# A fused adaLN, segment-memory attention and gated-MLP block: chunked weight loads, a rebuilt prologue and a fill rate per segment

## The chip, the cores and the metric

One Trainium2 chip, one core. The metric is device time in microseconds, lower is better: the median of several executions. Beside it there is one execution taken with the hardware profiler, which has a time of its own.

## The reference, cut to what matters

The block works on x of shape (1, 2048, 448): 16 heads of 28, four segments of 512 rows, and an MLP of width 1792. Everything is bf16 outside.

```python
mod = (silu(c) @ w_mod).reshape(1, 6, 1, -1)
sa, ca, ga, sb, cb, gb = mod[:, 0], mod[:, 1], ...
h = layernorm(x) * (1 + ca) + sa
q, k, v = h @ wq, h @ wk, h @ wv          # 4 segments, 16 heads
for s in range(4):
    p = softmax(q_s @ k_s.T * scale + causal_mask)
    a_dot = p @ v_s
    a_mem = (phi(q_s) @ M) / (phi(q_s) @ z + 1e-6)
    o_s = g * a_mem + (1 - g) * a_dot     # g = sigmoid(beta), per head
    M, z = M + phi(k_s).T @ v_s, z + phi(k_s).sum()
x = x + ga * (o @ wo)
h = layernorm(x) * (1 + cb) + sb
x = x + gb * ((sigmoid(h @ w_gate) * (h @ w_up)) @ w_down)
```

phi(t) is t + 1 above zero and exp(t) below.

## The kernel before, in words

All weights and all of x stay in SBUF. The work goes by the four segments of 512 rows (four tiles of 128 rows each). Heads go in four groups of four (hc), each head padded to 32 rows, so that one group fills 128 partitions.

The program is written in the order in which each engine shall run it; every engine (TensorE, VectorE, ScalarE, GpSimd called POOL, and SP, which only starts DMAs) takes its own instructions in that order and waits by semaphores. The order is made by hand in the main loop at the end. Its spine is the attention: for each segment s and head group hc three groups g of logits (`logits`, L386, with the exponential on ScalarE, L389, and the causal mask on POOL, L397), and after the first of them the product with v for the head group before (`pv`, L411, and L419 for the memory), with its ends on VectorE (L425 to L446). After each group `run_fill` takes other jobs from the queue `fill` until their costs, in ns, have used up the rate of that group. These jobs are the projections of q, k and v (`proj_qk` L311, `proj_v` L323), the memory update (`mem_update` L359), the Wo tiles (`wo_tile` L461, with the residual, L464, and the statistics of the second layer norm, L238), gate and up (`gate_up` L479 and L484) and down (`down` L493). A job has a planned cost: `MM, MV, TR = 216, 190, 60` ns for a matmul of 512 columns, one of 448, and a transpose. So a q or k projection costs 864, a v projection or a Wo tile 760, a gate/up pair 1728, a down tile 2660.

Work that should come some time later on another engine is put off by `later(ns, ...)`. A clock, counted up by the costs of what has been written so far, says when it is due; `need(tag)` forces what is not yet written. So a layer norm (`ln1_start`) is spread out: statistics at once, norm (L246) at 5200 to 6700, modulation (L257) at 14500 to 16000 ns after its start. For segments 2 and 3, and for the second layer norm, h is transposed by a DMA between the norm and the modulation (`norm_t`, L253, on SP); for segments 0 and 1 by TensorE (`pe_chunk`, L265 to L270). The transposes of phi(k) (L348) and of the attention's output (`otr`, L452), every load after the start and every store (L498) are SP's too, in one order.

The prologue loads x, the first two pieces of w_mod (`load_wm`, L113), wq, wk and wv, sets pads to zero on VectorE (L133 to L172), runs 24 warm-up matmuls (L562) on a zeroed tile, normalises segment 0, copies wq (ScalarE) and wk (VectorE) into the padded form (`pad_copy`, L573), computes two modulation vectors (`mod_cols`, L205, into `cp`) and transposes and modulates h (L265 to L270). Then two projections come, and the main loop. `load_wo` and the loads of w_gate, w_up and w_down are each one job of cost 0 in `fill`, with the two FFN matrices as one big DMA and one for the last 64 rows.

The rate of `run_fill` is 2400 ns for the first five head groups and (total − 15 × 2400) / 33 for the rest. The total leaves 9 gate/up jobs for the end (`TAIL_GU`). At the second head group of segments 1 to 3 the jobs of the segment before are added: four Wo tiles, what was left in the queue, down of the segment before that, the modulation (`h2_jobs`) and gate/up. After the loop the rest of the last two segments follows.

Of the kernel before, what the change touches and what calls it, by code (L numbers as in the profile page):

```python
# [17 lines left out]
def kernel(  # L18
# [34 lines left out]
    NWARM, TAIL_GU = 24, 9  # L53
# [13 lines left out]
    def m_f32(name):  # L67
        return ps_m.tile([P, 512], F32, tag="m", name=name)
# [32 lines left out]
    nc.sync.dma_start(c_col[:], c.rearrange("o (k p) -> p (o k)", p=KP))  # L101
    x_sb = const.tile([P, NSEG * TPS, D], BF16)

    def load_x(eng, t0, t1):
        eng.dma_start(x_sb[:, t0:t1, :], x_dram[t0 * P:t1 * P, :].rearrange("(t p) d -> p t d", p=P))

    load_x(nc.sync, 0, 2)
    load_x(nc.scalar, 2, 4)
    wmod_k = w_mod.rearrange("(k p) n -> p k n", p=KP)
# [30 lines left out]
    nc.vector.memset(wo_sb[:], 0.0)  # L140
    nc.vector.memset(wg_sb[LW:P, 3, :], 0.0)
    nc.vector.memset(wu_sb[LW:P, 3, :], 0.0)
# [15 lines left out]
    nc.gpsimd.memset(mhalf[:], -0.5)  # L158
    bmask = const.tile([P, NHC, 4, ME], BF16)
# [10 lines left out]
    qT_of = [const.tile([P, NHC, L], BF16, name=f"qT{s}") for s in range(3)]  # L170
    qT_of.append(qT_of[0])
    nc.vector.memset(qT_of[2][:, 0, :], 0.0)  # L172

# [3 lines left out]
    nc.vector.tensor_scalar(th[:], th[:], 0.5, 0.5, op0=ALU.mult, op1=ALU.add)  # L177
    silu = const.tile([KP, NK], BF16)
    nc.vector.tensor_tensor(silu[:], th[:], c_col[:], ALU.mult)
# [3 lines left out]
    def late_consts():  # L183
        nc.vector.tensor_copy(silu_bc[:], silu[:].rearrange("p (k o) -> p k o", o=1).to_broadcast([KP, NK, P]))
        for s in range(NSEG):
            nc.gpsimd.memset(vt_all[s][:, :, :, Dh:Dh + 1], 1.0)
        nc.scalar.activation(coef[:, 1, :], beta_t[:], AF.Tanh, scale=0.5)
        nc.vector.tensor_scalar(coef[:, 1, :], coef[:, 1, :], 0.5, 0.5, op0=ALU.mult, op1=ALU.add)
        nc.vector.tensor_scalar(coef[:, 0, :], coef[:, 1, :], -1.0, 1.0, op0=ALU.mult, op1=ALU.add)

        nc.gpsimd.memset(bmask[:], 1.0)
        for hs in range(4):
            nc.gpsimd.affine_select(out=bmask[:, :, hs, :], in_=bmask[:, :, hs, :], compare_op=ALU.is_ge,
                                    fill=0.0, base=-HP * hs, pattern=[[0, NHC], [0, ME]], channel_multiplier=1)
            nc.gpsimd.affine_select(out=bmask[:, :, hs, :], in_=bmask[:, :, hs, :], compare_op=ALU.is_ge,
                                    fill=0.0, base=HP * hs + Dh - 1, pattern=[[0, NHC], [0, ME]],
                                    channel_multiplier=-1)

    def mod_cols(jobs):
        cp = m_f32("cp")  # L200
        for j, vi in jobs:
            for kc in range(NK):
                for k in range(NK):
                    c0 = k * D + kc * P
                    nc.tensor.matmul(cp[:, vi * NK + kc:vi * NK + kc + 1], lhsT=wm[j][:, c0:c0 + P],  # L205
                                     rhs=silu[:, k:k + 1], start=(k == 0), stop=(k == NK - 1))
# [21 lines left out]
    class LN:  # L228
# [171 lines left out]
    def pv(s, hc):  # L400
# [24 lines left out]
        nc.vector.reciprocal(r1[:], accv[:, :, :, Dh])  # L425
        nc.vector.tensor_tensor(r1[:], r1[:], cb(0), ALU.mult)
# [14 lines left out]
        nc.vector.tensor_scalar(r2[:], memv[:, :, :, Dh], 1e-6, None, op0=ALU.add)  # L441
        nc.vector.reciprocal(r2[:], r2[:])
        nc.vector.tensor_tensor(r2[:], r2[:], cb(1), ALU.mult)
# [13 lines left out]
    def wo_tile(s, t):  # L457
# [12 lines left out]
        later(1500, lambda: ln.norm_t(t), ("ln2", s))  # L470

# [87 lines left out]
    wz = qT_of[2][:, 0, :]  # L559
    warm = ps_lg.tile([P, 4, 512], F32, tag="lg", name="warm")  # L560
    for _ in range(NWARM):
        nc.tensor.matmul(warm[:, 0, :], lhsT=ident[:], rhs=wz, start=True, stop=True)  # L562
    ln0 = LN([x_sb[:, t, :] for t in range(TPS)], ("1", 0))
    for t in range(TPS):
        ln0.stats(t)
    ln0.rstd(0, TPS)
    for t in range(TPS):
        ln0.norm(t)
# [36 lines left out]
    def load_wd():
        nc.sync.dma_start(wd_sb[:], B_w_down.rearrange("(fc p) n -> p fc n", p=P))

    fill.extend(sp(load_bw2) + j0[2:6] + sp(late_consts) + j0[6:10] + [ln1_start(2)] + j0[10:])
    fill.extend(sp(load_wo) + sp(load_wm3) + load_ffn(wg_sb, B_w_gate))
    fill.extend(ln1_pe_jobs(1) + m[0][0:1] + j1[:8] + [ln1_start(3)] + load_ffn(wu_sb, B_w_up) + m[1][0:1] + j1[8:] + [(1000, prep_b1)])  # L610
    fill.extend(sp(load_wd) + j2[:4] + m[0][1:] + j2[4:8] + [(2000, prep_b2)] + j2[8:] + m[1][1:])
# [5 lines left out]
    total = cost(fill) + sum(cost(wo_jobs(s) + h2_jobs(s) + gu_jobs(s)) for s in range(3)) \
        + sum(cost(down_jobs(s)) for s in range(2)) - TAIL_GU * 8 * MM
    early = 2400.0
    rate = lambda s, hc: early if s * NHC + hc < 5 else (total - 15 * early) / 33.0  # L620

    debt = 0.0
    for s in range(NSEG):
        for hc in range(NHC):
            prev = (s, hc - 1) if hc else (s - 1, NHC - 1)
            for g in range(3):
# [15 lines left out]
                debt = run_fill(rate(s, hc) + debt)  # L642
# [51 lines left out]
```

## Time and profile before

| | us |
|---|---|
| median of 3 runs | 284.12 (283.15 to 285.14) |
| the profiled execution, its own time | 282.85 |
| its span, from the first to the last instruction | 281.1 |
| TensorE (PE) busy | 250.8 |
| VectorE (DVE) busy | 187.4 |
| ScalarE (ACT) busy | 140.8 |
| GpSimd (POOL) busy | 70.8 |

All rows that follow are of the profiled execution, and their times count from its first instruction. PEld is TensorE's loading of weights, which runs beside its matmuls. SPq is the queue of SP. A row of the timeline has the start, the time that the merged instructions took, the engine, the line, the operation, output and inputs, the count, and in square brackets how long the engine had been idle before it and what released it. The granted clock is TensorE's, 1.00 for 2.4 GHz and 0.50 for 1.2 GHz.

### The profile page before, as it was taken

To read this page: it belongs to the slowest core of one execution; us is meant where nothing else is said; L and a number is where in the kernel's file an instruction comes from. 1 tells how busy PE (TensorE), PEld (TensorE's weight loads), DVE (VectorE), ACT (ScalarE), POOL (GpSimd) and SP (SyncE) were. 2 spreads that over 40 slices of the span, in tenths; PEclk is the share of its full clock that TensorE was granted. 3 is DMA by queue.
4 is the path that set the end of the run, shared out by engine and by line. 5 is a ranking of instruction groups with operands and counts; after the bars stand their busy time and mean duration, and the time that the engine had idled before them with its cause. 6 is when DMAs were issued, how large, how long until landed. Compare 5 with 4: busy or idle time off the path is not lost. (4 is left out here: it accounts for less than half of the span.)

```text
span 281.1 us, 5201 instructions
## 1 busy us (share of the span) xinstructions
PE 250.8 (89%) x2025; PEld 123.0 (44%) x2048; DVE 187.4 (67%) x426; ACT 140.8 (50%) x171; POOL 70.8 (25%) x127
## 2 busy tenths in 40 slices
PE   1989897983888999998797999889999999899995
PEld 0434453541453544544353554435545444344452
DVE  7578899910679778999655858976577493433321
ACT  2268798583365788765165667562662310133300
POOL 1109434331234034144312213521220040000000
PEclk9999998896699999999999999999999999999999
DMA  5998046699412001301211001141300012100001
GB/s 152 294 249 255 2 105 197 118 198 230 104 21 56 23 19 21 75 21 37 54 54 36 21 0 21 37 57 34 55 19 4 18 37 70 35 0 0 2 16 49
DMA packets 40848, 19.66 MB, mean 70 GB/s; under 512 B 29560, under 2 KB 39928, under 8 KB 40824
## 3 DMA queue, kind: packets, MB, share of 16 engines
q1 hardware_dynamic: 39608, 18.30, 29.2%
q10 hardware_dynamic: 1216, 1.03, 1.3%
q8 instruction: 16, 0.26, 0.4%
q14 instruction: 8, 0.07, 0.1%
HBM read 10.67 MB, written 1.84 MB: 44 GB/s over the span
## 5 line engine op out<-in xcount | busy, mean ns | idle before, releaser
L389 ACT ACTIVATE pT<-lg 128x2048 bf16<-128x2048 f32 (+1 forms) x48 | 76.5, 1594 | 48.6 <-PE lg L386 48.6
L397 POOL TENSOR_SCALAR_AFFINE_SELECT pT<-pT 128x512 bf16<-128x512 bf16 x64 | 43.9, 700 | 87.8 <-ACT pT L389 87.8
L487 DVE SCALAR_TENSOR_TENSOR fT<-tt,ups 128x512 bf16<-128x512 f32 x56 | 37.8, 683 | 35.9 <-PE ups L484 24.6
L479 PE MATMUL gps<-hT,wg_sb 128*128 128x512 bf16 x213 | 57.9, 380 | 3.5 <-DVE hT L257 2.6
L481 ACT ACTIVATE tt<-gps 128x512 f32<-128x512 f32 x56 | 33.0, 596 | 53.9 <-PE gps L479 49.4
L484 PE MATMUL ups<-hT,wu_sb 128*128 128x512 bf16 x219 | 56.6, 379 | 2.4 <-DVE t L439 1.5
L493 PE MATMUL dps<-wd_sb,fT 128*128 128x448 bf16 x224 | 44.2, 353 | 2.3 <-DVE fT L487 2.3
L484 PEld LDWEIGHTS <-wu_sb 128*128 128x128 bf16 x224 | 21.5, 98 | 30.1 <-DVE t L439 2.5
L479 PEld LDWEIGHTS <-wg_sb 128*128 128x128 bf16 x224 | 20.4, 97 | 28.9 <-issue 7.4
L493 PEld LDWEIGHTS <-fT 128*128 128x128 bf16 x224 | 21.4, 98 | 23.5 <-DVE fT L487 2.5
L497 DVE TENSOR_TENSOR ot<-dps,x_sb 128x448 bf16<-128x448 f32 x16 | 9.9, 622 | 23.3 <-PE dps L493 23.3
L411 PEld LDWEIGHTS <-pT 128*128 128x128 bf16 x640 | 18.4, 96 | 4.9 <-issue 2.0
L323 PE MATMUL pv<-wv_sb,hT 128*128 128x448 bf16 x64 | 14.7, 372 | 6.1 <-DVE kT L316 6.1
L238 DVE BATCH_NORM_STATS2 st<-x_sb 128x6 f32<-128x448 bf16 x32 | 19.7, 617 | 0.6
L311 PE MATMUL pq<-hT,wq_sb 128*128 128x512 bf16 x61 | 17.9, 391 | 2.5 <-DVE hT L257 1.3
L242 POOL TENSOR_SCALAR rs<-mv 128x1 f32<-128x1 f32 (+1 forms) x20 | 5.1, 255 | 59.0 <-DVE mv L239 59.0
L411 PE MATMUL acc<-vt,pT 128*128 128x29 bf16 x640 | 18.5, 175 | 1.4 <-ACT vt L325 1.4
L386 PE MATMUL lg<-qT,kT 28*128 28x512 bf16 (+3 forms) x256 | 17.6, 307 | 0.9 <-DVE kT L316 0.8
L311 PE MATMUL pq<-hT,wk_sb 128*128 128x512 bf16 x60 | 17.0, 392 | 1.1 <-ACT qT L314 0.7
L257 DVE TENSOR_SCALAR hT<-hT,cols 128x512 bf16<-128x512 bf16 x24 | 9.6, 447 | 12.4 <-DMA hT<-xn 12.3
L246 DVE TENSOR_SCALAR xn<-x_sb,mv,rs 128x448 bf16<-128x448 bf16 x32 | 15.3, 494 | 2.4 <-POOL rs L243 2.3
L243 POOL TENSOR_TENSOR rs<-rs,mhalf 128x1 f32<-128x1 f32 (+1 forms) x20 | 13.7, 683 | 1.7
(81 smaller groups left out, 232.6 us busy)
## 6 DMA issues: line engine op xcount, KB each, us to landing
wm<-in_w_mod_dram SPq DMA_DIRECT2D x5, 392.0 KB, 4.2
out_dram<-ot SPq DMA_DIRECT2D x16, 112.0 KB, 1.7
wd_sb<-in_B_w_down_dram SPq DMA_DIRECT2D x1, 1568.0 KB
x_sb<-in_A_x_dram SPq DMA_DIRECT2D x3, 448.0 KB, 5.5
wg_sb<-in_B_w_gate_dram SPq DMA_DIRECT2D x1, 1344.0 KB, 11.3
wu_sb<-in_B_w_up_dram SPq DMA_DIRECT2D x1, 1344.0 KB
wm<-in_w_mod_dram ACTq DMA_DIRECT2D x1, 392.0 KB, 6.1
wo_sb<-in_A_wo_dram SPq DMA_DIRECT2D x4, 98.0 KB
```

Source lines behind the costliest of these rows:

```text
L238: nc.vector.bn_stats(st[:], self.srcs[i])
L246: nc.vector.tensor_scalar(self.xn[:, i, 0:D], self.srcs[i], self.mv[:, i, 0:1], self.rs[:, i:i + 1], op0=ALU.subtract, op1=ALU.mult)
L311: nc.tensor.matmul(pq[:, 0:L], lhsT=head_cols(w_sb, k, hc), rhs=h[:, k, :], start=(k == 0), stop=(k == NK - 1))
L386: nc.tensor.matmul(lg[:, hs, wid:wid + nq], lhsT=kT[r, hc, kb * P:(kb + 1) * P], rhs=qT[r, hc, kb * P:L], start=True, stop=True, tile_posi ...
L389: nc.scalar.activation(pT[:, :, w0:w0 + wid], lg[:, :, 0:wid], AF.Exp, scale=scale)
L397: nc.gpsimd.affine_select(out=blk, in_=blk, compare_op=ALU.is_ge, fill=0.0, base=0, pattern=[[0, 4], [1, P]], channel_multiplier=-1)
L411: nc.tensor.matmul(accv[:, qb, hs, 0:ME], lhsT=pT[:, hs, c0:c0 + P], rhs=vt[:, kb, hc * 4 + hs, 0:ME], start=(kb == 0), stop=(kb == qb))
L479: nc.tensor.matmul(gp[:, 0:L], lhsT=wg_sb[:, k, fs], rhs=h[:, k, :], start=(k == 0), stop=(k == NK - 1))
L481: nc.scalar.activation(tt[:], gp[:, 0:L], AF.Tanh, scale=0.5)
L484: nc.tensor.matmul(up[:, 0:L], lhsT=wu_sb[:, k, fs], rhs=h[:, k, :], start=(k == 0), stop=(k == NK - 1))
L487: nc.vector.scalar_tensor_tensor(ft[:], tt[:], 1.0, up[:, 0:L], op0=ALU.add, op1=ALU.mult)
L493: nc.tensor.matmul(dp[:, 0:D], lhsT=fT_of[(s, fc)][:, t * P:(t + 1) * P], rhs=wd_sb[:, fc, :], start=(fc == 0), stop=(fc == NFC - 1))
```

## The change

Four parts. The prologue: c is loaded after x, the warm-up's tile is zeroed first, three memsets go from VectorE to POOL, the rstd is done for two tiles at a time, the modulation vectors and two more warm-ups come ahead of the transposes, the transposes go tile by tile, and a third projection stands ahead of the loop. The loads: w_gate and w_up are loaded in four chunks of 128 rows (the last of 64) each and w_down in four chunks, one after every second job (`spread`). The end of a Wo stage: from segment 2 on the Wo tiles alternate with the jobs that were left, and the modulation of the second layer norm is put off by 6500 to 7700 ns after the last Wo tile instead of standing in the queue after down. The fill rate: 2400 ns until the second head group of segment 1; from there it is fixed per segment, so that 4, 4 and 9 gate/up jobs are left when the segment ends. Besides, the two gates of the output are inverted once, with one small operation less per head group from segment 1 on.

```diff
...
-    NWARM, TAIL_GU = 24, 9
+    NWARM, EARLY, KEEP = (20, 2), 2400.0, (0, 4, 4, 9)
...
-    nc.sync.dma_start(c_col[:], c.rearrange("o (k p) -> p (o k)", p=KP))
...
     load_x(nc.sync, 0, 2)
     load_x(nc.scalar, 2, 4)
+    nc.sync.dma_start(c_col[:], c.rearrange("o (k p) -> p (o k)", p=KP))
...
+    wz = qT_of[2][:, 0, :]
+    nc.vector.memset(wz, 0.0)
...
-    nc.vector.memset(wo_sb[:], 0.0)
-    nc.vector.memset(wg_sb[LW:P, 3, :], 0.0)
-    nc.vector.memset(wu_sb[LW:P, 3, :], 0.0)
...
     nc.gpsimd.memset(mhalf[:], -0.5)
+    nc.gpsimd.memset(wo_sb[:], 0.0)
+    nc.gpsimd.memset(wg_sb[LW:P, 3, :], 0.0)
+    nc.gpsimd.memset(wu_sb[LW:P, 3, :], 0.0)
...
+        nc.vector.tensor_scalar(coef[:], coef[:], 1e-30, None, op0=ALU.max)
+        nc.vector.reciprocal(coef[:], coef[:])
...
-        nc.vector.reciprocal(r1[:], accv[:, :, :, Dh])
-        nc.vector.tensor_tensor(r1[:], r1[:], cb(0), ALU.mult)
+        nc.vector.tensor_tensor(r1[:], accv[:, :, :, Dh], cb(0), ALU.mult)
+        nc.vector.reciprocal(r1[:], r1[:])
...
-        nc.vector.tensor_scalar(r2[:], memv[:, :, :, Dh], 1e-6, None, op0=ALU.add)
+        nc.vector.scalar_tensor_tensor(r2[:], memv[:, :, :, Dh], 1e-6, cb(1), op0=ALU.add, op1=ALU.mult)
         nc.vector.reciprocal(r2[:], r2[:])
-        nc.vector.tensor_tensor(r2[:], r2[:], cb(1), ALU.mult)
...
         later(1500, lambda: ln.norm_t(t), ("ln2", s))
+        if t == TPS - 1:
+            for kc in range(NK):
+                later(6500 + 400 * kc, lambda kc=kc: ln.modulate(kc, 2), ("ln2", s))
...
-        def mods():
-            need(("ln2", s))
-            for kc in range(NK):
-                ln2_of[s].modulate(kc, 2)
-        return [(0, mods)]
+        return [(0, lambda: need(("ln2", s)))]
...
+    warm_up(NWARM[0])
+    ln0 = LN([x_sb[:, t, :] for t in range(TPS)], ("1", 0))
+    for t in range(TPS):
+        ln0.stats(t)
+        if t % 2:
+            ln0.rstd(t - 1, t + 1)
+        if t == 1:
+            silu_ops()
+    mod_cols(((0, 0), (1, 1)), False)
+    warm_up(NWARM[1])
+    pts = [m_bf16("lntr") for _ in range(NK)]
     for k in range(NK):
         pad_copy(nc.scalar, wq_sb, wq_st, k)
-        pad_copy(nc.vector, wk_sb, wk_st, k)
-    mod_cols(((0, 0), (1, 1)))
+    for t in range(TPS):
+        ln0.norm(t)
+        if t == 1:
+            for k in range(NK):
+                pad_copy(nc.vector, wk_sb, wk_st, k)
+            mod_evac(((0, 0), (1, 1)))
+        for kc in range(NK):
+            nc.tensor.transpose(pts[kc][:, t * P:(t + 1) * P], ln0.xn[:, t, kc * P:(kc + 1) * P], ident[:])
+    for kc in range(NK):
+        ln0.pe_evac(pts[kc], kc, 0)
...
-    for c, fn in j0[:2]:
+    for c, fn in j0[:3]:
...
+    early_loads = [load_wo, lambda: load_x(nc.sync, 3 * TPS, 4 * TPS), load_wm3] \
+        + [piece(wg_sb, B_w_gate, k) for k in range(NK)] + [piece(wu_sb, B_w_up, k) for k in range(NK)]
+    fill.extend(sp(load_bw2))
+    fill.extend(spread(j0[3:6] + sp(late_consts) + j0[6:10] + [ln1_start(2)] + j0[10:] + ln1_pe_jobs(1) + m[0][0:1]
+                       + j1[:8], early_loads, 2))
+    fill.extend([ln1_start(3)] + m[1][0:1] + j1[8:] + [(1000, prep_b1)])
+    fill.extend(spread(j2[:4] + m[0][1:] + j2[4:8] + [(2000, prep_b2)], [piece_wd(f, min(f + 4, NFC)) for f in range(0, NFC, 4)], 2))
+    fill.extend(j2[8:] + m[1][1:])
...
-                    fill.extend(wo_jobs(s - 1) + tail)
+                    for w in wo_jobs(s - 1):
+                        fill.append(w)
+                        if tail and s > 1:
+                            fill.append(tail.pop(0))
+                    fill.extend(tail)
...
+                    pace[0] = (cost(fill) - KEEP[s] * 8 * MM) / (12 if s < 3 else 9)
-                debt = run_fill(rate(s, hc) + debt)
+                debt = run_fill(pace[0] + debt)
...
```

`piece` loads 128 rows of a weight matrix, `piece_wd` four of the 14 blocks of w_down, both on SP; `spread(jobs, steps, 2)` puts one load after every second job.

## Rows read from the trace of the kernel before

**Rows 1.** The page's first part: busy us, share of the span, instructions.

```profile
PE 250.8 (89%) x2025; PEld 123.0 (44%) x2048; DVE 187.4 (67%) x426; ACT 140.8 (50%) x171; POOL 70.8 (25%) x127
```

**Rows 2.** Busy time by stages: stage, length, PE, PEld, DVE, ACT, POOL, clock, DMA, GB/s.

```profile
28.00:30.20 2.20, 1.12 (x18) 0.88 (x16) 2.13 (x7) 2.12 (x3) 1.35 (x3) 1.00 0.00 0
45.00:47.50 2.50, 1.18 (x7) 0.30 (x4) 2.35 (x8) 2.50 (x6) 1.52 (x2) 1.00 0.69 158
47.50:51.00 3.50, 3.24 (x10) 0.93 (x11) 3.39 (x7) 1.53 (x3) 2.23 (x4) 0.52 1.06 354
...
61.20:64.60 3.40, 2.04 (x52) 1.43 (x51) 0.00 (x0) 2.25 (x5) 0.63 (x1) 1.00 1.02 306
64.60:74.90 10.30, 4.68 (x29) 2.53 (x27) 4.12 (x13) 2.77 (x4) 1.22 (x2) 0.51 1.15 180
...
77.80:125.20 47.40, 44.87 (x415) 22.16 (x416) 40.49 (x91) 33.49 (x41) 14.95 (x24) 1.00 0.17 35
125.20:138.00 12.80, 10.16 (x100) 5.23 (x98) 12.00 (x30) 5.07 (x5) 6.27 (x13) 1.00 0.14 32
138.00:151.00 13.00, 11.40 (x105) 5.82 (x105) 7.53 (x18) 6.01 (x5) 3.59 (x6) 1.00 0.18 49
...
174.00:187.00 13.00, 11.29 (x104) 5.40 (x102) 11.92 (x29) 6.41 (x7) 5.85 (x12) 1.00 0.17 40
...
224.00:243.00 19.00, 17.69 (x90) 8.61 (x90) 11.77 (x26) 1.19 (x2) 3.31 (x8) 1.00 0.18 47
```

**Rows 3.** The timeline, VectorE and TensorE, around 70 us.

```profile
69.79 0.74 DVE L257 TENSOR_SCALAR hT<-hT,cols 128x512 bf16<-128x512 bf16 x2 [12.35 <-DMA hT<-xn]
...
71.18 1.65 PE L323 MATMUL pv<-wv_sb,hT 128*128 128x448 bf16 x4 [5.62 <-DVE kT L316]
```

**Rows 4.** The timeline, loads and transposes on SP and a norm, 44 to 65 us.

```profile
44.42 0.57 SPq L130 DMA_DIRECT2D wu_sb<-in_B_w_up_dram  x1
...
50.44 0.70 DVE L246 TENSOR_SCALAR xn<-x_sb,mv,rs 128x448 bf16<-128x448 bf16 x2
...
55.51 2.50 SPq L253 DMA_TRANSPOSE hT<-xn  x2
...
59.37 0.58 SPq L606 DMA_DIRECT2D wd_sb<-in_B_w_down_dram  x1
...
60.04 4.58 SPq L253 DMA_TRANSPOSE hT<-xn  x2
```

**Rows 5.** The waits of SP's queue: who, for what, us, times, longest.

```profile
SPq L348 <- DMA pk<-e: 6.1, 1, 6.1
```

**Rows 6.** The timeline of the prologue, and POOL's memset of bmask.

```profile
5.89 7.41 PE L562 MATMUL warm<-qT,ident 128*128 128x512 bf16 x24 [5.89 <-DVE th L177]
...
11.28 1.96 ACT L573 COPY wq_sb<-wd_sb 128x448 bf16<-128x448 bf16 x4 [6.26 <-DMA wd_sb<-in_A_wq_dram]
...
14.59 1.45 ACT L267 ACTIVATE hT<-lntr,cols 128x512 bf16<-128x512 bf16 x2 [1.34 <-PE lntr L265]
...
18.11 0.39 PE L386 MATMUL lg<-qT,kT 28*128 28x512 bf16 x4 [0.79 <-DVE kT L316]
...
23.07 0.79 POOL L191 MEMSET bmask<- 128x464 bf16 x1
```

**Rows 7.** The first two loads of w_mod (L113), time to landing.

```profile
DMA to landing us min/median/max: 6.1/7.2/8.3
```

**Rows 8.** The timeline around the Wo tiles of segments 0 and 1.

```profile
77.80 3.20 PE L461 MATMUL pwo<-wo_sb,oT 128*128 128x448 bf16 x16
...
88.50 0.70 DVE L246 TENSOR_SCALAR xn<-x_sb,mv,rs 128x448 bf16<-128x448 bf16 x1
...
91.74 1.86 DVE L257 TENSOR_SCALAR hT<-hT,cols 128x512 bf16<-128x512 bf16 x4
...
117.05 6.07 SPq L452 DMA_TRANSPOSE oT<-ou  x2
...
125.23 2.44 PE L461 MATMUL pwo<-wo_sb,oT 128*128 128x448 bf16 x12
```

More of the change, by code (lines that the diff above doesn't have):

```diff
@@ L108 @@
     load_x(nc.scalar, 2, 4)
+    nc.sync.dma_start(c_col[:], c.rearrange("o (k p) -> p (o k)", p=KP))
+    qT_of = [const.tile([P, NHC, L], BF16, name=f"qT{s}") for s in range(3)]
+    qT_of.append(qT_of[0])
+    wz = qT_of[2][:, 0, :]
+    nc.vector.memset(wz, 0.0)
     wmod_k = w_mod.rearrange("(k p) n -> p k n", p=KP)
@@ L168, with silu_ops @@
     coef = const.tile([P, 2, H], F32)
-    qT_of = [const.tile([P, NHC, L], BF16, name=f"qT{s}") for s in range(3)]
-    qT_of.append(qT_of[0])
-    nc.vector.memset(qT_of[2][:, 0, :], 0.0)
     th = const.tile([KP, NK], F32)
     nc.scalar.activation(th[:], c_col[:], AF.Tanh, scale=0.5)
-    nc.vector.tensor_scalar(th[:], th[:], 0.5, 0.5, op0=ALU.mult, op1=ALU.add)
     silu = const.tile([KP, NK], BF16)
-    nc.vector.tensor_tensor(silu[:], th[:], c_col[:], ALU.mult)
+    def silu_ops():
+        nc.vector.tensor_scalar(th[:], th[:], 0.5, 0.5, op0=ALU.mult, op1=ALU.add)
+        nc.vector.tensor_tensor(silu[:], th[:], c_col[:], ALU.mult)
     vt_all = [const.tile([P, TPS, H, ME + 1], BF16, name=f"vt{s}") for s in range(NSEG)]
@@ L197, in late_consts, with mod_cols @@
                                     channel_multiplier=-1)
-    def mod_cols(jobs):
-        cp = m_f32("cp")
+    cp_of = {}
+    def mod_cols(jobs, evac=True):
+        cp = cp_of[0] = m_f32("cp")
         for j, vi in jobs:
@@ L206, in mod_cols, with mod_evac @@
                                      rhs=silu[:, k:k + 1], start=(k == 0), stop=(k == NK - 1))
+        if evac:
+            mod_evac(jobs)
+    def mod_evac(jobs):
+        cp = cp_of[0]
         for j, vi in jobs:
@@ L265, in pe_chunk, with pe_evac @@
                 nc.tensor.transpose(pt[:, t * P:(t + 1) * P], self.xn[:, t, kc * P:(kc + 1) * P], ident[:])
+            self.pe_evac(pt, kc, vi, act)
+        def pe_evac(self, pt, kc, vi, act=True):
+            if kc == 0 and ("1", 0) == self.key:
+                self.h = new_hT(self.key)
             if kc % 2 and act:
@@ L556, in prep_b3, with warm_up @@
             later(1700 * fc + 800, lambda fc=fc: scale_w(wd_sb, fc, gb), "wd")
-    wz = qT_of[2][:, 0, :]
     warm = ps_lg.tile([P, 4, 512], F32, tag="lg", name="warm")
[L561 to L568, printed above, removed]
+    def warm_up(n):
+        for _ in range(n):
+            nc.tensor.matmul(warm[:, 0, :], lhsT=ident[:], rhs=wz, start=True, stop=True)
     def pad_copy(eng, dst, st, k):
@@ L581 @@
     ln1_start(1, True)[1]()
-    for kc in range(NK):
-        ln0.pe_chunk(kc, 0)
     tick(0)
     j0, j1, j2, j3 = [proj_jobs(s) for s in range(NSEG)]
-    for c, fn in j0[:2]:
+    for c, fn in j0[:3]:
         fn()
@@ L601, in load_wm3, with piece, piece_wd, spread @@
     def load_wm3():
-        load_x(nc.sync, 3 * TPS, 4 * TPS)
         wm[3] = load_wm(nc.sync, 3)
[L605 to L611, printed above, removed]
+    def piece(w_sb, w, k):
+        r = min(P, D - k * P)
+        return lambda: nc.sync.dma_start(w_sb[0:r, k, :], w[k * P:k * P + r, :])
+    def piece_wd(f0, f1):
+        src = B_w_down.rearrange("(fc p) n -> p fc n", p=P)
+        return lambda: nc.sync.dma_start(wd_sb[:, f0:f1, :], src[:, f0:f1, :])
+    def spread(jobs, steps, every):
+        steps, res = list(steps), []
+        for i, j in enumerate(jobs):
+            res.append(j)
+            if i % every == every - 1 and steps:
+                res.append((0, steps.pop(0)))
+        assert not steps
+        return res
+    early_loads = [load_wo, lambda: load_x(nc.sync, 3 * TPS, 4 * TPS), load_wm3] \
[6 more added lines that the diff above has]
+    fill.extend(j2[8:] + m[1][1:])
     fill.extend(j3)
@@ L615, in cost @@
         return sum(cst for cst, _ in jobs)
[L617 to L620, printed above, removed]
+    pace = [EARLY]
     debt = 0.0
@@ L634 @@
                     tail = list(fill)
+                    print("left", s, cost(tail), len(tail))
                     fill.clear()
-                    fill.extend(wo_jobs(s - 1) + tail)
+                    for w in wo_jobs(s - 1):
[3 more added lines that the diff above has]
+                    fill.extend(tail)
                     if s >= 2:
```

2 lines of the change are left out of this document (removed).

## The prediction

> **What bounds the kernel now.** I read the page first, then the busy time by stages, then the timeline where a stage is not full, then the queue of SP. The page's first part [rows 1] has TensorE busy for 250.8 of 281.1 us and VectorE for 187.4: TensorE is the engine that ends the run, but 30 us of the span are not its own. The stages [rows 2] say where. The reader is to take the busy time of TensorE from the length of each stage and to look at the granted clock beside it. From 77.8 on there are only small holes, each at the end of a segment: 2.6 us in 125.2 to 138.0, 1.6 in 138.0 to 151.0, 1.7 in 174.0 to 187.0, 1.3 in 224.0 to 243.0. The big one is before: in 61.2 to 64.6 TensorE has 2.04 us of 3.4, and in 64.6 to 74.9 it has 4.68 of 10.3 at a mean clock of 0.51, the lower level, 1.2 GHz. A second, smaller one is 45.0 to 51.0: 1.18 of 2.5 us, then 3.24 of 3.5 at 0.52.
>
> The timeline names the cause of the big hole [rows 3]. VectorE sits idle for 12.35 us, until 69.79, and is released by the DMA that writes hT from xn; it is the modulation of segment 3 (L257), and VectorE works in order, so the casts and the softmax ends behind it wait too. TensorE waits 5.62 us for a kT cast that stands behind it. That hT is late by the queue of SP [rows 4]: the last two normalised tiles of segment 3 are there at 51.1, but their four transposes are issued from 55.51 to 64.6, two of them behind the load of w_down (one instruction, 1568 KB, at 59.37). Ahead of that SP stood 6.1 us on a pk transpose [rows 5] that had been queued behind the load of w_up (44.42). So two whole-tensor loads in one queue with the transposes make a VectorE stall, and this makes a TensorE stall and a fall of its clock.
>
> **The change part by part, on the profiled execution (282.85 us, span 281.10).**
>
> *Loads.* The order of the jobs hardly changes; what changes is where the loads stand among the transposes. Added up from the job costs (864 ns a q or k projection, 760 a v, 450 a logits group, 1100 a pv), ln1_start(3) plus 5200 to 6700 ns falls inside the v projections of segment 1 and the first projection of segment 2, in both kernels. Before, w_down stood ahead of the first projection of segment 2, so between the second and third transpose. After, its first chunk stands behind the second projection: all four transposes are ahead. w_up goes as four chunks of 448 KB or less between projections of segment 1, the first ahead of all transposes. Bytes are the same, there are 7 more issues on SP of 0.58 us each (the row at 59.37), where SP has no other work; w_gate and w_up are first read behind the Wo tiles of segment 0 (77.80, [rows 8]). So the transposes can go out as the tiles come, from 47 to 53, and land by 56; VectorE reaches the modulation at 57.4. What goes: the idle time, 1.36 (61.2 to 64.6) and 5.62 (64.6 to 74.9), and half of the 4.68 us that ran at the lower level, 2.3: **9.3 us**. Bounds: 3.5, if SP is still held up, half of the idle time stays and the clock falls all the same; 9.3. I take 9.3, as no large load is left between those tiles. What is late next is TensorE's own work. The hole at 45.0 to 51.0 is not touched: VectorE is 2.35 of 2.5 us busy there, and its order is the same (0, at best its 1.3 + 1.6 = 2.9).
>
> *Prologue.* Before, the last modulated chunk of h is there at 14.59 + 1.45 = 16.04 [rows 6], because ScalarE first copies wq (lands 11.28, copies end 13.24) and then waits until TensorE, busy with warm-up matmuls until 5.89 + 7.41 = 13.30, has made cp and the transposes. After, the memset for the warm-ups is VectorE's first, so they start at about 1.5 (an estimate: the instructions ahead of them end there) and, at the same 0.31 each, 20 end at about 7.7. cp then waits for wm0, which lands 8.3 us after its issue at 1.8, so 10.1 [rows 7]; cp's small matmuls take about 1, tiles 0 and 1 are ready, the wk copies (0.8) and tiles 2 and 3 (0.7) follow until about 12.1, the wk load allowing, and ScalarE can do its two chunks at 13.24 to 14.7. Gain 1.3. The third projection ahead of the first logits fills most of the 0.79 us that those wait for kT (18.11): 0.8. Against it: three memsets go to POOL ahead of the rstd. Its memset of 464 columns took 0.79, so three of 1792 take at most 9.2 and end at 10.6 (none hurts below 6.5); then rstd and norms are 1 to 2 us later. And TensorE, idle from 7.7 to 10.1 and thin to 13, may start its projections at the lower clock: 12 matmuls of 0.216 (the planner's MM) twice as long, minus 2.6. Bounds −2.6 to +2.1; I take **+1.0**. The coef lines add two 128x32 operations once (under 0.5, VectorE) and take 12 small ones away (0.2 each): nothing on the path.
>
> *Fill rate.* Before, every group from segment 1 on got 2890 ns of fill. After it is, with the job costs, about 2400 in segment 1, 3090 in segment 2, 3250 in segment 3: two gate/up jobs and one memory update move from segment 1 to 2, one gate/up from the last stretch forward. TensorE's work is the same. In 77.8 to 125.2 TensorE works 44.87 and VectorE 40.49; after it is about 40.5 against 37.5, VectorE 93% full, where it was 90%. In 28.0 to 30.2 and 45.0 to 51.0, as full, TensorE lost 1.1, 1.3 and, with the clock, 1.9. I charge **−1.0** (bounds 0 and −4).
>
> *Wo among gate/up.* Four Wo tiles in a row give VectorE more (add, statistics, norm) than TensorE (0.8 each); in 125.2 to 138.0 and 174.0 to 187.0 VectorE is busy for 12.00 of 12.8 and 11.92 of 13.0 [rows 2], and TensorE has its holes there. Spread, each has a gate/up beside it (1.73 by the planner). First hole 2.6 to about 0.3; but Wo of segment 1 now follows its last pv by 7.6 us of jobs instead of 8.6, and oT was in time by little (issue ends 123.1, TensorE starts at 125.23 [rows 8]): new wait 0 to 2, I take 1. **+1.3**. Second hole 1.7 to 0.5: **+1.2**.
>
> *Modulation by the clock.* The four modulations of h2 no longer stand after the third down (or the last) but 6500 ns after the last Wo tile. This ends the 1.6 in 138.0 to 151.0 and most of the 1.3 in 224.0 to 243.0: **+1.6, +1.1**. Now they may be queued on VectorE before their transposes have landed, with fT, ot and pv ends behind them. Segment 0's landed 91.7, which is 10.7 us after the last Wo tile (77.80 + 3.20) [rows 8]; VectorE was late there: the last tile's norm, asked for 1.5 us after its Wo tile, ran at 88.50, 7.5 after it. So it gets to the modulations no earlier. Later ones have a shorter chain. 0, at worst 4 each.
>
> Sum: 9.3 + 1.0 − 1.0 + 1.3 + 1.2 + 1.6 + 1.1 = 14.5. The profiled execution would come to 268.35; it was 1.27 under the median 284.12, so **269.6 us**, with a range of its own of 266 to 273.
>
> **The rivals.**
> 1. *The clock falls in the prologue.* For: after the waits of 45.0 to 47.5 and 61.2 to 64.6 the granted clock did fall to half [rows 2], and the new prologue has TensorE idle for 2.4 us and thin for 2 more. Against: 28.0 to 30.2 has a hole too (1.12 of 2.2), and kept its clock. It takes the prologue from +1.0 to −1.6: 272.2. The Trainium skill has this rule (TensorE: Matmul & The Clock Gate, "HAM oscillation — how this bites in real kernels"): a wait on a DMA between bursts of matmuls sends the engine back to its slow clock, and the next burst starts cold. By that rule the time is 272.2, without it 269.6; the two holes of the trace agree.
> 2. *SP is still late.* Chunks stand between transposes, and pk, oT and hT share the queue; if SP is again held, half of the idle time stays (3.5) and all of the clock's fall (2.3), so 9.3 becomes 3.5: 275. For: [rows 5]. Against: the largest load between those transposes is then none, and the pieces are a quarter of the old ones.
> 3. *It doesn't do what it says.* The same bytes pass, and the transposes wait for them wherever they stand: only the small terms, some of which go to VectorE's load: 283.
> 4. *Slower: modulations ahead of their transposes.* VectorE works in order; if all four segments' modulations wait the full 10.7 − 6.5 = 4.2 us, TensorE loses 16.8, the 2.7 of that edit are gone as well, and it is 284.1 − 11.8 + 16.8 = 289. It decides from 3 us a segment on. For: 6.5 is under 10.7. Against: VectorE's own lateness of 6 us in the same place.
> 5. *Better:* the new rhythm also closes 45.0 to 51.0: 2.9 more, 266.7.
>
> **How the numbers follow.** Forecast 0.50, rival 1 0.15, rival 2 0.14, rival 3 0.07, rival 4 0.06, rival 5 0.08. Range 264.5 to 277: it takes in the forecast, rivals 1, 2 and 5 and the bounds of the small terms, and leaves out rivals 3 and 4 (0.13). Faster by over 1% (2.8 us, about what a measurement of this kernel tells from no change): 0.87; within 1%: 0.07; slower: 0.06.
>
> **What would show it.** Right: no VectorE wait for hT of more than 2 us before 80; clock 1.0 from 55 on; TensorE's stage that ends with the first Wo tile some 10 us earlier; no hole after the third down. Wrong: a wait of L257 on its DMA in several segments (rival 4); granted clock at half during the first projections (rival 1); SP issuing segment 3's transposes after 55 (rival 2); or new TensorE waits of several us in segment 1, which would mean that VectorE has become the bound there.

## The result, and the profile after

The changed kernel took **274.4 us** (median of 4 runs, 273.08 to 275.80), the kernel before 284.01 on the same chip (283.15 to 285.14); the ratio is 0.966, 95% interval 0.960 to 0.972. That is faster, by 9.6 us where 14.5 were forecast (269.6), inside the range of 264.5 to 277. The profiled execution took 275.80, the longest of the four.

The page's first part of the changed kernel has TensorE as busy as before [rows 1] and VectorE 6 us less:

```profile
PE 250.6 (91%) x2021; PEld 122.9 (45%) x2046; DVE 181.4 (66%) x413; ACT 140.7 (51%) x171; POOL 73.9 (27%) x132
```

The stages where TensorE is not full are still mostly at the start; of the holes that [rows 2] had behind 125, those around the second Wo and the third down are nearly gone, and some 2 us around segment 1's Wo tiles stay (113 to 129). One fall of the clock has moved: 47.5 to 51.0, which [rows 2] had at 0.52, is at 1.00, and behind a wait of TensorE for hT at 30.52 (1.58 us) the clock falls, to 0.63 in 30.5 to 34.0, where it had been full. Columns: stage, its length, TensorE busy, granted clock, DMA share, GB/s.

```profile
7.30:9.85 2.55, 0.00 (x1) 1.00 1.12 260
9.85:14.80 4.95, 3.38 (x50) 0.61 1.13 264
14.80:19.00 4.20, 4.20 (x12) 0.64 1.14 251
...
62.40:65.20 2.80, 0.02 (x1) 1.00 0.63 154
65.20:69.30 4.10, 4.06 (x56) 0.58 1.09 140
...
75.10:77.00 1.90, 0.45 (x3) 1.00 0.36 74
...
113.00:129.00 16.00, 13.90 (x127) 1.00 0.16 36
129.00:140.00 11.00, 10.73 (x103) 1.00 0.32 40
...
175.00:188.00 13.00, 12.73 (x115) 1.00 0.20 42
```

Two things stand there that the forecast had only as rivals: the clock at half in the prologue, and what is left of the big hole. The timeline of the changed kernel, TensorE, VectorE and SP, shows the second:

```profile
49.08 6.24 SPq L365 DMA_TRANSPOSE pk<-e  x2
53.09 1.00 PE L376 MATMUL dM<-vt,pk 128*128 128x116 bf16 x16
...
56.06 2.50 SPq L265 DMA_TRANSPOSE hT<-xn  x2
59.92 2.56 SPq L265 DMA_TRANSPOSE hT<-xn  x2
63.85 0.73 DVE L269 TENSOR_SCALAR hT<-hT,cols 128x512 bf16<-128x512 bf16 x2 [5.12 <-DMA hT<-xn]
65.24 1.36 PE L340 MATMUL pv<-wv_sb,hT 128*128 128x448 bf16 x4 [2.83 <-DVE kT L333]
67.08 2.50 SPq L634 DMA_DIRECT2D wd_sb<-in_B_w_down_dram  x3
70.19 2.51 SPq L468 DMA_TRANSPOSE oT<-ou  x2
76.49 1.74 PE L477 MATMUL pwo<-wo_sb,oT 128*128 128x448 bf16 x7 [1.38 <-DMA oT<-ou]
```

VectorE's wait for hT is 5.12 us where it was 12.35 [rows 3], TensorE's 2.83 where it was 5.62, and the clock falls once more behind it. The transposes of segment 3 still leave SP only from 56.06 on, hardly other than in [rows 4]. The row ahead of them tells why: two pk transposes occupy SP for 6.24 us, until 55.32; an issue takes 1.2 us (a single pk transpose of E1, below, has 1.22), so the second goes out at 54.1, when the dM matmuls, which read pk, end (53.09 + 1.00). pk has one buffer (`bufs=1`), so segment 1's transpose has to wait until segment 0's data are read. The trace of before has the same two rows (SP until 54.78, less 1.2 is 53.58; dM until 53.55), and the reading in the forecast, a queue behind w_up, overlooked the second. That reading was not false: the 6.1 us of [rows 5] for a DMA into pk end at about 53.1 (45.64, an issue of 1.35, 6.1). But dM ends just behind it, and in the changed kernel, where SP waits only 1.6 us for that DMA, SP still stands until dM ends. The last two rows here are for later:

```profile
45.64 9.14 SPq L348 DMA_TRANSPOSE pk<-e  x2
...
52.36 1.19 PE L359 MATMUL dM<-vt,pk 128*128 128x116 bf16 x16
...
92.86 1.17 PE L479 MATMUL gps<-hT,wg_sb 128*128 128x512 bf16 x4
...
94.73 1.15 PE L411 MATMUL acc<-vt,pT 128*128 128x29 bf16 x40
```

Last, oT: three chunks of w_down stand on SP ahead of two oT transposes (67.08, 70.19), these take 5.4 and 6.3 us to land, where those of pk took 2.4 to 4.1, and TensorE waits 1.38 us at the first Wo tiles.

### The profile page after: what moved, and what is told of

Same layout as the page of the kernel before. It is cut to its first block, busy times and chain, and to the rows that moved or that the text cites. A ratio compares the mean times of both kernels' runs of the same rounds, so it can differ in the third digit from the quotient of the medians.

```text
span 274.1 us, 5199 instructions
## 1 busy us (share of the span) xinstructions
PE 250.6 (91%) x2021; PEld 122.9 (45%) x2046; DVE 181.4 (66%) x413; ACT 140.7 (51%) x171; POOL 73.9 (27%) x132
## 3 DMA queue, kind: packets, MB, share of 16 engines
q10 hardware_dynamic: 1216, 1.03, 1.3%
## 4 chain that ended last, share of the span: by engine, by line
PE 47%; DVE 21%; issue 3%; DMA 3%; POOL 2%; ACT 1%; SPq 1%; DVEq 0%; ACTq 0%
PE gps L498 13%; PE dps L512 13%; PE ups L503 12%; DVE st L250 3%; PE acc L428 3%; DVE x_sb L480 3%; DVE fT L506 3%; PE lg L403 2%; DVE xn L258 2%; DMA oT<-ou 2%; DVE wd_sb L562 1%; POOL rs L255 1%; PE pv L340 1%; PE pwo L477 1%; DVE mv L251 1%
## 5 line engine op out<-in xcount | busy, mean ns | idle before, releaser
L414 POOL TENSOR_SCALAR_AFFINE_SELECT pT<-pT 128x512 bf16<-128x512 bf16 x64 | 42.4, 680 | 63.3 <-ACT pT L406 63.3
L498 PE MATMUL gps<-hT,wg_sb 128*128 128x512 bf16 x215 | 57.4, 380 | 0.5
L254 POOL TENSOR_SCALAR rs<-mv 128x1 f32<-128x1 f32 (+2 forms) x21 | 5.1, 244 | 74.8 <-DVE mv L251 73.0
L428 PE MATMUL acc<-vt,pT 128*128 128x29 bf16 x640 | 19.1, 177 | 0.6 <-POOL pT L414 0.5
L258 DVE TENSOR_SCALAR xn<-x_sb,mv,rs 128x448 bf16<-128x448 bf16 x32 | 16.7, 541 | 2.9 <-POOL rs L255 2.8
L477 PE MATMUL pwo<-wo_sb,oT 128*128 128x448 bf16 x64 | 14.3, 354 | 2.3 <-DMA oT<-ou 1.4
L333 DVE CAST kT<-pq 128x512 bf16<-128x512 f32 x16 | 10.7, 681 | 6.4 <-PE pq L328 6.4
```

Of the source, the lines that this page charges most:

```text
L258: nc.vector.tensor_scalar(self.xn[:, i, 0:D], self.srcs[i], self.mv[:, i, 0:1], self.rs[:, i:i + 1], op0=ALU.subtract, op1=ALU.mult)
L414: nc.gpsimd.affine_select(out=blk, in_=blk, compare_op=ALU.is_ge, fill=0.0, base=0, pattern=[[0, 4], [1, P]], channel_multiplier=-1)
L428: nc.tensor.matmul(accv[:, qb, hs, 0:ME], lhsT=pT[:, hs, c0:c0 + P], rhs=vt[:, kb, hc * 4 + hs, 0:ME], start=(kb == 0), stop=(kb == qb))
L498: nc.tensor.matmul(gp[:, 0:L], lhsT=wg_sb[:, k, fs], rhs=h[:, k, :], start=(k == 0), stop=(k == NK - 1))
```

## The experiments

All are the changed kernel with one edit, unless it is said otherwise. Kernels that were measured together share their runs of before (medians 283.5 for E1 to E4, 283.0 for E6 to E9, 284.7 for the rest), so the ratio to before is what is compared; 0.01 of it is 2.84 us. The last column is the distance to the changed kernel by the ratios; with the two intervals put together it is good to about 2.3 us.

| | edit | median (range) | ratio, interval | us against the changed kernel |
|---|---|---|---|---|
| E1 | own pk buffers | 271.78 (269.48 to 272.12) | 0.957 [0.952, 0.962] | −2.5 |
| E2 | whole loads | 279.48 (278.30 to 280.87) | 0.987 [0.982, 0.992] | +5.9 |
| E3 | whole loads, own pk | 276.44 (275.39 to 277.89) | 0.976 [0.971, 0.980] | +2.7 |
| E4 | c first | 271.52 (271.13 to 272.33) | 0.958 [0.955, 0.962] | −2.2 |
| E6 | 30 warm-ups | 272.36 (271.84 to 273.14) | 0.961 [0.955, 0.967] | −1.4 |
| E7 | old fill rate | 273.56 (273.15 to 274.72) | 0.967 [0.961, 0.972] | +0.2 |
| E8 | modulations as a job | 280.13 (279.02 to 282.13) | 0.990 [0.986, 0.993] | +6.7 |
| E9 | Wo in a row | 275.39 (274.73 to 276.18) | 0.973 [0.967, 0.978] | +1.9 |
| E5 | E1 and E4 | 269.62 (268.98 to 270.83) | 0.949 [0.944, 0.954] | −4.8 |
| E10 | E1, E4 and E6 | 269.69 (268.35 to 270.14) | 0.949 [0.944, 0.953] | −4.9 |
| E11 | old prologue | 277.86 (275.08 to 278.20) | 0.977 [0.972, 0.982] | +3.2 |
| E12 | E5, w_down from ScalarE | 273.50 (272.42 to 274.17) | 0.963 [0.958, 0.968] | −0.9 |

**E1, E2, E3: is it the loads or the buffer?** The buffers of E1 are four tiles of the fT ring, which is empty at that time:

```diff
-            pk_of[s] = pipe.tile([P, NHC, TPS, P], BF16, tag="pk", bufs=1, name="pk")
+            if s == 1:
+                pk_of[s] = [pipe.tile([P, L], BF16, tag="fT", bufs=NFC + 2, name="fT")[:].rearrange("p (t q) -> p t q", q=P)
+                            for _ in range(NHC)]
+            else:
...
```

E2 puts the load lines of before back; E3 has both edits.

> The changed kernel, with segment 1's transposed phi(k) in four buffers of its own, so that its second transpose no longer waits until the state update of segment 0 has read the one pk buffer. Buffer theory (SP is held by pk's write-after-read, 49.08 to 54.13 in the changed kernel): segment 3's four hT transposes are issued by about 54 where they went out from 56.1 to 61.2, VectorE's wait of 5.1 us that ended at 63.85 falls under 1, TensorE's 2.8 before 65.2 goes, and the granted clock stays full from 55 to 75 (about 1.7 more): 270. Rival (the bytes ahead of the transposes hold them, wherever the buffer is): nothing changes, 274.

> The changed kernel with w_gate, w_up and w_down loaded whole again at their old places; one pk buffer. Both theories: VectorE's wait grows back to about 12 us, the clock falls for longer, and the time rises by what the chunks brought, 3.5 to 5: 278 to 279. If it is below 275.5, the chunks were worth nothing, and the gain came from the other edits.

> Whole loads at their old places and four own buffers for segment 1's pk. Buffer theory: SP gets past pk at about 49, two of segment 3's transposes go out before w_down and two behind its 1568 KB, so VectorE's wait is 2 to 5 us in place of 12: 272 to 275, that is well under the whole loads with one buffer. Rival (bytes): as with one buffer, 278 to 279.

The timeline of E1, SP (pk's second part is now named fT), VectorE and TensorE:

```profile
48.67 1.22 SPq L370 DMA_TRANSPOSE pk<-e  x1
...
51.94 2.50 SPq L265 DMA_TRANSPOSE hT<-xn  x2
54.54 1.97 SPq L370 DMA_TRANSPOSE fT<-e  x1
56.60 2.52 SPq L265 DMA_TRANSPOSE hT<-xn  x2
60.42 0.92 DVE L269 TENSOR_SCALAR hT<-hT,cols 128x512 bf16<-128x512 bf16 x2 [1.86 <-DMA hT<-xn]
60.55 2.44 PE L340 MATMUL pv<-wv_sb,hT 128*128 128x448 bf16 x12
```

The first two hT transposes go out 4.1 us earlier, the last two 3.3, behind a phi(k) transpose that occupies SP for 1.97 us (54.54), 0.8 more than an issue. The profile names VectorE's phi(k) for that, but the one that this transpose reads was ready at 52.66 (a row of VectorE has it at 52.23, 0.43 long); what held it is open. VectorE waits 1.86, TensorE not at all: its 12 pv matmuls run in one piece where the changed kernel had the 2.83. The time is 2.5 us less (271.8; 270 was expected). With whole loads the same buffers bring 3.2 (E3 against E2), so the rival, by which they change nothing, falls: each of the two gains is little more than 2.3, but they agree, and in E1 the trace shows the way. E3 itself came out at 276.4, above the 272 to 275 that were expected, and VectorE's wait is still 8.34 us there, not 2 to 5. But E2 shows that the chunks count as well, with one pk buffer 5.9, with four 5.3 (E3 against E1). Here is why, in the timeline of E2:

```profile
45.63 9.72 SPq L365 DMA_TRANSPOSE pk<-e  x2
...
53.76 0.38 PE L376 MATMUL dM<-vt,pk 128*128 128x116 bf16 x4 [2.67 <-DMA pk<-e]
...
71.50 1.65 PE L340 MATMUL pv<-wv_sb,hT 128*128 128x448 bf16 x4 [5.51 <-DVE kT L333]
```

A transpose behind the whole w_up lands late, so dM waits 2.67 us for pk, and the transpose that waits for dM goes later still; then w_down stands between the hT transposes. Both theories are half of the answer: the loads make the data late, and the single buffer hands that on to everything queued behind it on SP.

**E4, E6, E11: the prologue.** E4 puts the load of c ahead of x again, E6 has `NWARM = (30, 2)`, E11 has the whole prologue of before. In E11 the third projection goes back into the queue, so that the loads that are spread up to w_up also stand one job earlier; the two were not tried apart.

> The changed kernel with the load of c ahead of x on SP again, as before the change; nothing else. Theory that c's place costs the prologue: c lands at about 4.8 in place of 6.95, VectorE's 1.6 us on th goes, w_q lands about 1 us earlier (12.66 now, 11.28 before the change), the first logits start about 1 us earlier, 273.4. Rival: x comes later by as much, and the clock's fall during the first projections stays, so less than 0.4 us changes, 274.

> The changed kernel with 30 warm-up matmuls in place of 20, so that TensorE is busy nearly until wm0 lands; c still behind x. Theory that the idle time ahead of cp (2.6 us, from 7.23) drops the clock: the granted clock stays full from 7 to 19, the first q, k and q projections take 1.0 us each where two of them took 2.00 and 1.63, the first logits start about 1.5 us earlier than 19.01, and the time is 272.9. Rival (the first logits wait for w_q, which lands at 12.66 whatever the clock): less than 0.5 us, 274.

> The changed kernel with the prologue of before (c first, memsets of w_o, w_gate and w_up on VectorE, 24 warm-ups behind them, one rstd, modulations behind the copies, two projections ahead of the first logits), all else as changed. My forecast gave the new prologue 1.0: without it 275.4. Theory by the trace (the first logits come 0.9 us later than before, and the clock falls in the projections): the new prologue costs 1 to 1.6, so 273.

In the changed kernel c lands behind x, at 6.95; in E4 at 4.92. The timeline of the changed kernel, then of E4, and one stage, of E4 and of E7, which has c behind x like the changed kernel:

```profile
6.95 0.21 ACT L176 ACTIVATE th<-c_col 112x4 f32<-112x4 bf16 x1 [2.70 <-DMA c_col<-in_c_dram]
...
12.66 1.96 ACT L583 COPY wq_sb<-wd_sb 128x448 bf16<-128x448 bf16 x4 [5.51 <-DMA wd_sb<-in_A_wq_dram]
...
19.01 0.40 PE L403 MATMUL lg<-qT,kT 28*128 28x512 bf16 x4
```

```profile
4.92 0.20 ACT L176 ACTIVATE th<-c_col 112x4 f32<-112x4 bf16 x1 [0.71 <-DMA c_col<-in_c_dram]
...
10.16 0.95 PE L212 MATMUL cp<-silu,wm 112*128 112x1 bf16 x32 [1.45 <-DMA wm<-in_w_mod_dram]
...
11.36 1.96 ACT L583 COPY wq_sb<-wd_sb 128x448 bf16<-128x448 bf16 x4 [6.24 <-DMA wd_sb<-in_A_wq_dram]
```

```profile
14.80:19.00 4.20, 4.20 (x22) 1.00 1.14 227
```

```profile
14.80:19.00 4.20, 3.52 (x18) 1.00 1.14 250
```

The copies of wq start 1.3 us earlier, as expected, and the first logits 2.25 (16.76). Not all of that is c's place, as the clock stays full in that run. It does so from 9.85 to 19.0 in E3 and E7 as well, with c behind x, and their first logits start at 17.75 and 18.11, only 1.0 and 1.35 after E4's. In E5, which has c first, it falls (0.54 in this stage), and they start at 18.84, hardly ahead of the changed kernel's 19.01. The time is 2.2 less, about the border of what the two intervals tell from nothing, where 1 was expected and the rival said less than 0.4; E5 against E1, the same edit, gives 2.3 again. So c first is a gain; how much of it is the clock's stays open.

E6 did not do what it was meant to. TensorE is idle for 0.56 us ahead of cp in place of 2.62, and the clock falls all the same, only later. Its timeline and the stage:

```profile
10.79 0.95 PE L212 MATMUL cp<-silu,wm 112*128 112x1 bf16 x32 [0.56 <-DMA wm<-in_w_mod_dram]
...
16.05 1.86 PE L328 MATMUL pq<-hT,wk_sb 128*128 128x512 bf16 x4
17.70 1.91 PE L328 MATMUL pq<-hT,wq_sb 128*128 128x512 bf16 x4
```

```profile
14.80:19.00 4.20, 3.76 (x11) 0.65 1.13 248
```

The first logits come at 19.55, no earlier; what E6 gains (1.4, not surely above nothing) lies elsewhere: the wait for hT at 30 us is 0.74 in place of 1.58, the clock does not fall behind it (1.00 in 30.5 to 34.0), and the wait for oT at the first Wo tiles is 0.24 in place of 1.38. The Trainium skill (TensorE: Matmul & The Clock Gate, "HAM oscillation — how this bites in real kernels") says that a wait on a DMA between bursts sends the engine to its slow clock. The changed kernel agrees (2.62 us of wait, then 0.61 and 0.64); E4, with 1.45 us there, and E7, with 2.05, kept their clock, and E6, with 0.56, did not, so that wait alone does not decide it here.

E11 went against the trace reading. The first logits of the changed kernel start 0.9 us later than in [rows 6], from which a loss was expected; undoing the prologue loses 3.2 more. With the old prologue in the same kernel they start at 18.92: the 24 warm-ups took 8.22 us there and 7.41 in [rows 6], and with them the first logits' start moves by 0.8 from run to run of the same prologue. At the same start the new prologue has one projection (1.0 us) more behind it. In the rest of the difference the profile shows pieces only: TensorE's waits at 65.84 (3.14) and for oT at 76.75 (1.89) are 0.3 and 0.5 longer than in the changed kernel.

**E7, E8, E9: the later edits.** E7 sets `pace[0] = 2890.0`; E8 takes out the modulations by the clock and puts `mods` back into h2_jobs; E9 takes out

```diff
-                        if tail and s > 1:
-                            fill.append(tail.pop(0))
```

> The changed kernel with 2890 ns of fill for every group from segment 1's second chunk on, as before the change, in place of about 2400, 3090 and 3250 by segment. My forecast charged the new rates 1.0 us (bounds 0 and 4): with the old one 273.4. Rival: the old rate puts more on VectorE in segment 1 than TensorE has time for, and leaves the last segment short of fill, so the new rates were a gain: 275.5 or more.

> The changed kernel with the four modulations of h2 as a job behind the third down (or behind Wo) again, not 6500 ns after the last Wo tile. My forecast gave that edit 1.6 + 1.1: without it 277.1, with a hole of about 1.5 us on TensorE behind the third down of two segments. Rival: the place of the modulations no longer matters once Wo stands among gate/up: 274.4 to 275.

> The changed kernel with the Wo tiles of segments 1 and 2 four in a row again, ahead of the gate/up jobs. My forecast gave that edit 1.3 + 1.2: without it 276.9, with holes of about 2.6 and 1.7 us around the Wo tiles. Rival: most of the holes came from the modulations or from the late start, so less than 1 us: 274.4 to 275.3.

E7: no difference that can be told. E9: 1.9, less than the two intervals resolve; its timeline has two waits of TensorE, where 2.5 us in all were forecast (the changed kernel has 0.67 and 0.86 around the first place and none of 0.5 at the second). E9 has another 0.41 at the first place, so the waits there are 1.6 against 1.5, and only the second place shows a gain:

```profile
125.00 1.04 PE L498 MATMUL gps<-hT,wg_sb 128*128 128x512 bf16 x4 [1.19 <-DVE t L456]
...
173.12 1.04 PE L503 MATMUL ups<-hT,wu_sb 128*128 128x512 bf16 x4 [1.17 <-DVE t L456]
```

E8 costs 6.7, more than twice the 2.7, and mostly at another place. Of the two forecast holes the last is there, a wait of 1.03 at 240.14; behind the third down there is none; and the largest is at segment 0's first gate/up. Its timeline and stage:

```profile
87.99 1.15 PE L428 MATMUL acc<-vt,pT 128*128 128x29 bf16 x40
89.18 0.17 DVE L442 TENSOR_TENSOR r<-acc,coef 128x16 f32<-128x16 f32 x1 [1.40 <-PE acc L428]
...
91.90 2.00 DVE L269 TENSOR_SCALAR hT<-hT,cols 128x512 bf16<-128x512 bf16 x4
...
92.68 0.39 PE L495 MATMUL gps<-hT,wg_sb 128*128 128x512 bf16 x1 [2.99 <-DVE hT L269]
```

```profile
92.70:97.00 4.30, 4.06 (x11) 0.65 0.15 34
```

VectorE does a whole end of softmax (from 89.18, for which it waits on TensorE) ahead of the modulations; TensorE waits 2.99 us and the clock falls for 4 more. In the kernel before, the same job cost nothing at this place, because the order was another: gate/up (92.86) stood ahead of the next pv (94.73, both shown above), and so the modulations (91.74, [rows 8]) ahead of its softmax end. E7 has that order too (gate/up at 88.96, pv at 91.36), at the old rate of 2890 ns; at about 2400 pv comes first, in E8 at 87.99. So E8 measures the old place of the modulations together with the new rate. In the changed kernel the modulations stand first, at the price of a short wait for the DMA, and gate/up follows with none:

```profile
90.98 1.39 DVE L269 TENSOR_SCALAR hT<-hT,cols 128x512 bf16<-128x512 bf16 x4 [1.31 <-DMA hT<-xn]
...
91.52 1.28 PE L498 MATMUL gps<-hT,wg_sb 128*128 128x512 bf16 x4
```

**E5, E10, E12: putting it together.**

> The changed kernel with two of the edits tried alone: four buffers of its own for segment 1's pk, and the load of c first on SP. If the two costs are independent, their gains add: 274.4 - 2.6 - 2.9 = 268.9. Rival (both only shift when TensorE waits and when its clock falls, and share that): 271 to 271.5, no better than either alone.

> As the kernel with both edits (own pk buffers, c first), and 30 warm-up matmuls in place of 20. If the idle time ahead of cp still costs something once c is first: about 1 us less, 268. Rival (the extra matmuls stand ahead of cp in TensorE's order and only fill the idle time): as without them, 268.9.

> Own pk buffers, c first, and the four chunks of w_down issued by ScalarE's queue in place of SP's, so that the oT transposes of segment 0's last chunks don't stand behind them. Theory that their place on SP makes TensorE's wait for oT at the first Wo tiles (1.38 us in the changed kernel, 0.8 to 1.4 in the others): 268.9 - 0.8 = 268.1. Rival (the transposes wait for the bytes, whichever queue they are in, or ScalarE's 4 issues delay its exponentials): 268.9 or more.

E5 gains 4.8, where E1 and E4 add up to 4.7: the two are independent as far as the intervals tell, and its interval lies under that of the changed kernel. E10 keeps the clock full in the prologue (1.00 in 14.8 to 19.0, 0.54 in E5) and starts the first logits 2.0 us ahead of E5 (16.87 against 18.84), and is no faster. The timelines of E5 and E10 tell where most of that went, to the wait for oT at the first Wo tiles:

```profile
71.53 2.29 PE L482 MATMUL pwo<-wo_sb,oT 128*128 128x448 bf16 x10 [0.73 <-DMA oT<-ou]
```

```profile
70.66 2.29 PE L482 MATMUL pwo<-wo_sb,oT 128*128 128x448 bf16 x10 [2.09 <-DMA oT<-ou]
```

E10 comes to the first Wo tile 2.2 us ahead (68.02 against 70.24) and leaves this wait 0.9 ahead.

In E12 that wait is gone, but TensorE comes to these matmuls 3.2 us later (74.74 against 71.53), and the last oT transpose goes out later too, at 69.64, where E5's have gone by 68.7. So E12 does not show what the chunks' place on SP costs. It loses 3.9 us against E5. Its timeline, ScalarE's queue, ScalarE and TensorE, and the stage behind:

```profile
55.57 0.37 ACTq L639 DMA_DIRECT2D wd_sb<-in_B_w_down_dram  x1
55.99 0.59 ACT L331 CAST qT<-pq 128x512 bf16<-128x512 f32 x1 [4.48 <-DMA hT<-xn]
...
56.63 1.02 PE L328 MATMUL pq<-hT,wk_sb 128*128 128x512 bf16 x4 [1.19 <-ACT qT L331]
...
64.24 3.15 PE L340 MATMUL pv<-wv_sb,hT 128*128 128x448 bf16 x8 [2.20 <-DVE kT L333]
```

```profile
62.00:66.00 4.00, 1.80 (x6) 0.50 0.99 202
```

The first chunk left at 47.63. The second leaves only at 55.57, and the casts behind it on ScalarE stand still for 4.48 us. What held it, the profile puts down to the hT transposes; that was not tried by itself. And hT is late again, with three chunks sent off at 55.57 to 57.4, while SP sends off the last hT transposes (54.31 to 56.85; DMA share 1.09 in 56 to 62, 0.70 in E5): TensorE waits 2.20 and its clock falls. The Trainium skill (DMA: Bandwidth & Descriptors, "Issuing engines are not separate DMA queues") says that DMAs share the same 16 engines whoever starts them, and only the time to start them is saved. The run is in line with it, as the move gained nothing, and adds that an engine with work of its own stood still behind such a start, for 4.48 us.

## Why the prediction was right or wrong

**Direction and range right, 4.8 us too low.** By its own signs the way that the forecast took did not come true: VectorE waits 5.12 us for hT, not under 2, the clock is at 0.58 in 65.2 to 69.3, not full from 55 on, segment 3's transposes go out after 55, and the first Wo tile comes at 74.56, 3.2 us earlier and not 10. Only the hole after the third down went as it said. The range held because it had been drawn wide enough for rivals 1 and 2. The terms, as forecast and as each edit costs when it alone is undone:

| edit | forecast | undone alone |
|---|---|---|
| loads in chunks | 9.3 | 5.9 (E2) |
| prologue | 1.0 | 3.2 (E11) |
| fill rate | −1.0 | 0.2, not told from 0 (E7) |
| Wo among gate/up | 1.3 + 1.2 | 1.9 (E9) |
| modulations by the clock | 1.6 + 1.1 | 6.7 (E8) |
| sum | 14.5 | 17.9; all together 9.7 |

- **The step that failed** is the one on SP: "Ahead of that SP stood 6.1 us on a pk transpose [rows 5] that had been queued behind the load of w_up", and "the transposes can go out as the tiles come, from 47 to 53". They went out from 56.06 to 62.5. The row of [rows 5] names the DMA pk<-e, and rightly for those 6.1 us, but the transpose behind it went out as dM ended, and did so again when that DMA cost SP only 1.6 us. That wait is for the buffer, and no placing of loads removes it. So half of TensorE's wait stayed (2.83 of 5.62), and the fall of the clock (4.06 us at 0.58). That is rival 2, "SP is still late", in what it does and nearly in its time (275), with a cause that it did not name. The nearness in time is partly luck, since 275 has the other terms as forecast, and they came out otherwise. The term of 9.3 measured 5.9; E1 takes the cause away and gains 2.5 more.
- **Prologue.** Rival 1's sign was there (the clock at half in the first projections), but its conclusion does not follow: with that fall, the new prologue still is worth 3.2. The forecast named neither the place of c, which costs 2.2 (E4; the clock's share in that is open), nor that the first logits' start moves between runs of the same code.
- **Modulations by the clock** was right in its direction, "they may be queued on VectorE before their transposes have landed", and that this costs little (VectorE waits 1.31 us in segment 0 and 0.95 at 140.49, TensorE not at all for it); rival 4 did not come. Its size does not compare: the place that costs most in E8, the first gate/up of segment 0, was not among the two that were priced, as it had no hole before. The hole comes from the old place of the modulations and the new fill rate together, and the forecast priced the two apart. Of the two places that it did price, E8 has the last (1.03, forecast 1.1) and not the one behind the third down.
- **The sum.** Adding terms read from one trace was itself a mistake. Single undos come to 17.9 where all five together are 9.7: edits act on each other, as the last point shows for the rate, and a wait that one edit shortens can come back at the next transfer, as E10 shows. Each single figure is also only good to about 2.3.
- **New waits** came where a transfer had been hidden: oT at the first Wo tiles, 1.38 us, behind three chunks of w_down on SP. The forecast had asked that question for segment 1's oT (the 1 us within the Wo term) and not for segment 0's.

E5 beats both kernels: 269.6 us, 0.949 of before.

## What to carry to other kernels

When a queue stands on an instruction, ask for both of its ends: the data it reads, and the buffer it writes; compare the moment it goes out with the end of the last reader of that buffer before believing the name in the wait. A queue that works in order hands one such wait to all that is behind it, so a single-buffered tile in a queue shared with the critical transposes is worth a buffer before loads are rearranged. Undo edits one at a time to find what each is worth, and do not expect the parts to add up to the whole; where two edits set one order, as the rate and the place of the modulations do here, undo them together too.

## What was not expected of the hardware

One program's executions differ, and mostly with the clock that they were granted. The changed kernel took 275.80, 275.02, 273.79 and 273.08 us at mean granted clocks of 0.975, 0.980, 0.987 and 0.987; E1 took 269.48 at 0.998 and 271.64 to 272.12 at 0.981 to 0.987. The mean clock does not explain all of it: E7's shortest execution, 273.15, had its lowest, 0.975. Nor does the code settle where the clock falls: with the same prologue it was at 0.61 and 0.64 in 9.85 to 14.8 and 14.8 to 19.0 of the changed kernel, and at 1.00 in both in E3 and E7. The same 20 warm-up matmuls, started at the same 1.41, took 5.82 us in the changed kernel's profile and 7.30 in E4's. A difference of 1 to 2 us in the prologue between two single profiles is therefore no evidence.
